# A gated-attention and mixture kernel: where the D parts of the hidden tiles are made, and how attention units overlap

## Chip, core and metric

The kernel runs on one core of a Trainium2 chip. The metric is the device time of one execution in microseconds. Before the change it is 1072.71 us, the median of three runs from 1072.09 to 1073.56.

## What is computed

The first half is a gated linear recurrence. For each of 4 batches and 8 heads, over 768 positions of dimension 48:

```
state = alpha[t][:, None] * state + outer(k[t], v[t])
y[t]  = q[t] @ state
```

The second half takes y as 3072 rows of 384 numbers and runs four experts over all of them:

```
p = domain_probs / (domain_probs.sum(-1) + 1e-9)
for e in range(4):
    h = max(x @ w1[e], 0)            # 384 -> 1024
    out += p[:, e] * (h @ w2[e])     # 1024 -> 384
```

Everything is in fp32.

## The kernel before

**Attention units.** The recurrence is done in blocks of 128 positions. One block of one batch is a unit, attention(u), and there are 24 of them, ordered by block first and batch second. attention() is a generator of 17 steps (0 to 16), and each `yield` ends one. Steps 0 to 2 transpose alpha, k and q (`tp`), and step 1 also forms the products q*k (`own`, `dot`). Steps 3 to 6 begin the levels of a doubling scheme: ScalarE copies q (copy_q), VectorE multiplies q, the decay and k (next_q, next_k). Step 6 also fills the diagonal tile `near`. Step 7 makes the first scores, 32 matmuls on levels 0 to 3, and VectorE takes the results over masks (take). Steps 8 to 10 continue the levels. Step 11 makes the last scores (`far` and two more levels). Steps 12 and 13 copy `far` and `near` into `lat`. Step 14 transposes the keys back into AT. Step 15 is result(): matmuls on `lat`, v, q and the state into `yps`, copied to x_raw. Step 16 updates the state: matmuls into `sps`, then two VectorE operations on each half of the partitions. From the first block to the last but one a unit has such an update.

**Groups and experts.** The units are put in seven groups: the first two units, five groups of four, the last two. Group gi of the mixture covers the rows of its units. In this text gi is counted from 0. While the experts of group gi run, the attention units of the next group are worked on; while group 4 runs, the units of groups 5 and 6. The experts of groups 5 and 6 run without attention beside them.

**Layer 1.** up(gi, e, fc) makes one of eight hidden tiles of 128 features by up to 512 rows. From group 1 on, weights and x are split in three parts, so that fast matmuls give nearly fp32 results: six matmuls into `one` and three into `two`, in a ring of four PSUM banks. ScalarE scales `one` into t and VectorE adds `two` (L553). From group 2 on, the hidden tile is split as well (hidden_parts): ScalarE makes the top part, VectorE the low part (L580), and make_dif the D part, top/4096 - low (L590). These steps are put behind the matmuls of the next tile, so on VectorE the order is low and D of tile k-1, then the addition of tile k.

**D parts before.** With 512 rows, hidden_parts makes D for the first 256 columns at once, in layer 1. The second 256 go to the queue `later`, which down() empties.

**Layer 2.** down(gi, e, slots, between) multiplies hidden tiles with w2. From group 2 on, one call takes two slots of 128 rows, so a full group needs two calls, here called first and second. A call has 48 matmuls, n = 0 to 47: n = 0 to 31 use the top and low parts, tiles 0 to 5 ahead of 6 and 7, and n = 32 to 47 use the D parts, the eight tiles of the first slot and then those of the second. At each n with n % 4 == 3 one entry of `later` is made. add_up() accumulates the sums: for the first slot behind n = 29 and n = 39, for the second behind n = 31 and n = 47. In expert 0 the accumulation behind n = 29 and n = 31 is ScalarE's. In the last expert of a group, split_x() for the next group stands between the matmuls: ScalarE's part at the start of the first call, three pairs of VectorE operations (L248, L249) at n = 2, 12 and 22 of the second.

**The order.** It is written out by hand (manual_schedule), and every engine runs its instructions in the order of the program. A planner decides where attention steps go: up() and down() advance a clock by an estimated cost (advance, cost), and deal() gives each step of each unit a due time on that clock. deal() gives the units of a group an equal `space`, lets a unit last twice that, and puts its steps at the shares of its duration that BEATS lists. wanted[gi] is the moment when group gi's rows must be there, and MARGIN is kept ahead of it.

The buffers that bind steps of neighbouring units are `near` and `lat` (one each), the decay tile of the last level dec6 (one), four blocks of q, five tiles KT, and in PSUM two banks for scores, two for `tp`, `yps` and `sps`, four for the mixture.

Of the kernel before, what the change touches and what calls it, by code (L numbers as in the profile page):

```python
# [10 lines left out]
F32 = mybir.dt.float32  # L11
# [9 lines left out]
def kernel(  # L21
# [37 lines left out]
    nc = tc.nc  # L59

    B, H, S, D = q.shape
    E, DM, F = moe_w1.shape
    P = 128
    NCB = S // P
    NP = H // 2
    HD = 64
# [4 lines left out]
    NT = B * P  # L71
# [10 lines left out]
    j = np.arange(P)[:, None] % HALF  # L82
    n = np.arange(QUAD)[None, :]
# [7 lines left out]
    work = ctx.enter_context(tc.tile_pool(name="work", bufs=2))  # L91
    hid = ctx.enter_context(tc.tile_pool(name="hid", bufs=2))
    ps = ctx.enter_context(tc.tile_pool(name="ps", bufs=2, space=bass.MemoryType.PSUM))
# [18 lines left out]
    half = B // 2  # L112
    groups = [order[:half]] + [order[i:i + B] for i in range(half, len(order), B)]
    LAST = len(groups) - 1
# [16 lines left out]
    def raw(u, nm):  # L131
        return values[u % 2] if nm == "v" else apart[nm] if u == 1 else early[nm]
# [6 lines left out]
    splitting = []  # L139
    stores = deque()  # L140
    late = deque()
    later = deque()
    shared = {}
    accs = {}


    BEATS = [*(0.055 * (j + 1) for j in range(11)), 0.69, 0.75, 0.8, 0.87, 0.94, 1.0]
    MARGIN = 6.0
    waiting = deque()
    clock = 0.0  # L150
# [109 lines left out]
    def halves(t, m):  # L260
        return t.rearrange("p a (b two r) -> p a b two r", two=2, r=m)
# [7 lines left out]
    def attention(u):  # L269
        cb, b = units[u]  # L270
        ra, rk, rq, rv = (raw(u, nm) for nm in ("a", "k", "q", "v"))
# [39 lines left out]
        def next_q(li):  # L311
            m = LEVELS[li]
            qv = halves(QT, m)[:, :, :, 1, :]
            dv = halved(decs[li])
            nc.vector.tensor_mul(qv, qv, spread(dv[:, :, :, 0], m))  # L315
            dec = work.tile([P, NP, P // (2 * m)], F32, name=f"dec{li}", bufs=1)
            nc.vector.tensor_mul(dec, dv[:, :, :, 0], dv[:, :, :, 1])
            decs.append(dec)

# [33 lines left out]
        for li in range(3):  # L353
            copy_q(li)
            next_q(li)
            next_k(li)
            yield
# [29 lines left out]
        for r in range(NP // 2):  # L387
            for s in range(2):
                nc.tensor.matmul(far[HALF * s:HALF * (s + 1), r],  # L389
                                 lhsT=KTs[6][:, 2 * r + s, :HALF], rhs=qbs[6][:, 2 * r + s],  # L390
                                 start=True, stop=True)
# [7 lines left out]
        parts = lat.rearrange("p (r s i) c -> p r s i c", s=2, i=2)  # L399
        for s in range(2):  # L400
            rows = slice(HALF * s, HALF * (s + 1))
            nc.scalar.copy(out=parts[:HALF, :, s, :, HALF:], in_=far[rows])
        yield
        for s in range(2):
            rows = slice(HALF * s, HALF * (s + 1))
# [4 lines left out]
        st = sts[b]  # L410
# [47 lines left out]

        if cb < NCB - 1:
            KB = AT  # L460
            sps = ps.tile([P, NP, 2, D], F32, name="sps", tag="w")
            for p in range(NP):
                nc.tensor.matmul(sps[:, p], lhsT=KB[:, p, :], rhs=rv[:, 2 * p:2 * p + 2, :D],  # L463
                                 start=True, stop=True)
            for i in range(2):
                rows = slice(HD * i, HD * (i + 1))
                old, add = st[rows, :, i, :], sps[rows, :, i, :]
                if cb == 0:
                    nc.vector.tensor_copy(out=old, in_=add)
                else:  # L470
                    nc.vector.tensor_mul(old, old, decs[-1][rows].broadcast_to([HD, NP, D]))
                    nc.vector.tensor_add(old, old, add)
# [103 lines left out]
    def hidden_parts(x, parts):  # L576
        top, low, dif = parts
        nc.scalar.activation(out=top, in_=x, func=ACT.Relu, scale=TRIM)  # L578
        yield
        nc.vector.scalar_tensor_tensor(out=low, in0=x, scalar=0.0, in1=top.bitcast(F32),  # L580
                                       op0=ALU.max, op1=ALU.subtract)

        n = x.shape[-1]
        at = n // 2 if n == NT else 0
        if at:
            make_dif(*(part[:, :at] for part in parts))
        later.append([part[:, at:] for part in parts])

    def make_dif(top, low, dif):
        nc.vector.scalar_tensor_tensor(out=dif, in0=top.bitcast(F32), scalar=1 / 4096.0,  # L590
                                       in1=low.bitcast(F32), op0=ALU.mult, op1=ALU.subtract)
# [5 lines left out]
    def down(gi, e, slots, between):  # L597


        first = first_piece(gi, e)  # L600
        halves_ = split2(gi, e)
        if slots[0] == 0 and makes[1](gi, e):
            making.extend(split_piece(1, first + k) for k in range(NQ))
        if slots[0] == 0 and makes[0](gi, e) and 0 < e < E - 1:
            making.extend(split_piece(0, first + k) for k in range(2, NQ))
        sums = [[ps.tile([P, DM], F32, name=f"ops{j}", tag="g", bufs=4)
                 for j in range(2 if halves_ else 1)] for _ in slots]

        kinds = [((0, 1), range(FCH - 2)), ((0, 1), range(FCH - 2, FCH)), ((2,), range(FCH))]
        steps = [(part, i, fc) for parts, tiles in (kinds if halves_ else [((3,), range(FCH))])  # L610
                 for part in parts for i in range(len(slots)) for fc in tiles]
        for n, (part, i, fc) in enumerate(steps):
            c, f = divmod(fc, FPQ)
            h = hidden[c][:, :, f, slots[i] * P:(slots[i] + 1) * P]
            advance(cost(1, gi, e) / FCH / (3 if halves_ else 1))
            while between and n >= between[0][0] * len(steps):
                between.popleft()[1]()
            if n == len(steps) // 2:
                background()
            if later and n % 4 == 3:  # L620
                make_dif(*later.popleft())
            if halves_:
                w = wt[1][first + c].rearrange("p t (c d) -> p t c d", d=DM)[:, part, f]
                nc.tensor.matmul(sums[i][part // 2], lhsT=h[:, part], rhs=w,  # L624
                                 start=(fc == 0 and part != 1), stop=(fc == FCH - 1 and part != 0))
            else:
                w = wt[1][first + c].rearrange("p (c d) -> p c d", d=DM)[:, f]
                nc.tensor.matmul(sums[i][0], lhsT=h[:, 2].bitcast(F32), rhs=w,  # L628
                                 start=(fc == 0), stop=(fc == FCH - 1))
            if part >= 1 and fc == FCH - 1:  # L630
                add_up(gi, e, slots[i], part // 2, sums[i][part // 2 if halves_ else 0])
        while between:
            between.popleft()[1]()
        background()
        if slots[-1] == len(groups[gi]) - 1 and gi != LAST - 1:
            while makes[1](gi, e) and (making or splitting):
                background()

            for c in range(NQ):
                del wt[1][first + c]  # L640
                if c < NQ // 2 or gi == LAST:
                    load_piece(1, first + NQ + c)
                else:
                    late.append(first + NQ + c)
# [25 lines left out]
    def cost(layer, gi, e):  # L670
        n = len(groups[gi]) / 4
        if layer == 0:
            return 2.1 * n if split1(gi, e) else 2.6 * n
        return 4.1 if split2(gi, e) else 5.4

    def deal():

        wanted = [0.0]  # L680
        ends = [0.0, 0.0]
        events = []
        t = 0.0
        for (gi, e), after in zip(tasks, tasks[1:]):
            part = 1 - 1 / len(groups[0]) if gi == e == 0 else 1
            t += cost(0, gi, e) * FCH * part
            if after[1] == 0:
                wanted.append(t)
            t += cost(1, gi, e) * len(groups[gi]) * part

        for gis in [*([gi] for gi in range(1, LAST - 1)), [LAST - 1, LAST]]:
            gi, due = gis[0], wanted[gis[-1]] - MARGIN
            n = sum(len(groups[i]) for i in gis)
            first = wanted[gi - 1] if gi > 1 else 0.0
            space = (due - first) / (n if gi > 1 else (n + 1) / 2)
            if gi == 1:
                space /= 2
            for k in range(n):
                u = sum(map(len, groups[:gi])) + k
                end = due - (n - 1 - k) * space  # L700
                begin = max(end - 2 * space, ends[-2])
                ends.append(end)
                run = attention(u)
                events += [(begin + (end - begin) * beat, u, run) for beat in BEATS]
        return sorted(events, key=lambda x: x[:2])

    def advance(spent):
        nonlocal clock
        clock += spent
        while waiting and clock >= waiting[0][0]:  # L710
            next(waiting.popleft()[2], None)

    with tc.manual_schedule():
# [48 lines left out]
        for (gi, e), after in zip(tasks, [*tasks[1:], (None, None)]):  # L762
# [6 lines left out]
            for k, slots in enumerate(turns):  # L769

                between = deque()
                if after[1] == 0:
                    for step, at in enumerate((0.0, 0.52, 0.62, 0.72)):
                        at = at * len(turns) - k
# [33 lines left out]
```

## Time and profile before

| | before |
|---|---|
| median of three runs | 1072.71 us |
| the profiled execution | 1073.32 us |
| its span, first to last instruction | 1071.6 us |
| mean granted TensorE clock | 0.998 |
| groups 2, 3, 4 of the mixture, with attention | 374.6 to 880.5 us |
| VectorE busy in group 2, 3, 4 | 132.75 of 166.1, 136.25 of 169.5, 133.33 of 170.3 us |

A row of the profile's groups gives line, engine, operation, what is written and read, shapes, count, then busy time and mean duration, then idle time ahead of it and what ended that. Timeline rows begin with the start in us and the time the merged instructions take; in square brackets stands an idle time ahead and its releaser. Rows of waits read: engine, waiting tile and line, what it waited for, total us, how often, the longest. TensorE matmuls overlap, so the distance between starts is what one costs, not its duration, and an fp32 matmul shows as two records.

### The profile page before, as it was taken

What the parts mean: (1) busy time and instruction counts of PE and PEld (TensorE: products, weight loads), DVE (VectorE), ACT (ScalarE), POOL (GpSimd) and SP (SyncE); (2) the same over time, 40 slices, a digit from 0 to 9 for tenths busy, and PEclk for the clock granted to TensorE, in tenths of its full rate; (3) what the DMA queues carried; (4) which work ended last, traced back from release to release, by engine and by line L of the source; (5) the groups of instructions that cost most, each with busy time, mean ns of one, the idle gap of its engine ahead of it and who ended that gap; (6) DMA issues with size and microseconds to landing.
All of it is one profiled execution on the core that took longest, in us unless ns stands there. A gap on an engine that the chain in (4) does not pass through costs nothing.

```text
span 1071.6 us, 21614 instructions
## 1 busy us (share of the span) xinstructions
PE 1048.1 (98%) x8460; PEld 899.1 (84%) x8460; DVE 775.2 (72%) x1711; ACT 566.7 (53%) x1202; POOL 32.7 (3%) x71
## 2 busy tenths in 40 slices
PE   8899999999999999999999999999999999999998
PEld 8777777676776798898898898898889889898988
DVE  5488776656566978778877777986787866666565
ACT  5687866575656554536546445555464543323232
POOL 2010000000000100000000000000000000000000
PEclk9999999999999999999999999999999999999999
DMA  8597699687696967758759558586594543544540
GB/s 123 156 330 216 230 328 368 238 328 241 236 309 209 402 216 274 281 160 312 268 170 359 204 187 337 186 281 234 158 358 173 221 192 147 207 177 178 187 181 31
DMA packets 158838, 251.67 MB, mean 235 GB/s; under 512 B 120112, under 2 KB 135344, under 8 KB 136208
## 3 DMA queue, kind: packets, MB, share of 16 engines
q1 hardware_dynamic: 149600, 208.82, 57.1%
q0 software_dynamic: 5760, 41.29, 9.8%
q8 instruction: 67, 1.10, 0.4%
q10 hardware_dynamic: 3376, 0.17, 0.3%
q14 instruction: 35, 0.29, 0.1%
HBM read 207.79 MB, written 42.47 MB: 234 GB/s over the span
## 4 chain that ended last, share of the span: by engine, by line
PE 83%; DVE 8%; ACT 6%; issue 2%; DMA 1%; SPq 0%; DVEq 0%; ACTq 0%
PE ops L624 25%; PE one L540 21%; PE ops L628 10%; PE two L540 10%; PE sc L334 6%; PE yps L428 3%; PE tp L266 3%; PE one L532 2%; ACT qb L308 2%; PE far L389 1%; PE sps L463 1%; DVE near L344 1%; DVE t L553 1%; DVE hT L580 1%; DVE hT L590 1%
## 5 line engine op out<-in xcount | busy, mean ns | idle before, releaser
L624 PE MATMUL ops<-w,hT 128*128 128x384 f32 x1728 | 318.0, 339 | 4.4 <-DVE acc L658 4.3
L624 PEld LDWEIGHTS ops<-w,hT 128*128 128x128 f32 x1728 | 299.1, 188 | 9.9 <-DVE acc L658 5.6
L540 PE MATMUL one<-xT,w 128*128 128x512 f32 x960 | 253.8, 400 | 2.6 <-DVE xT L248 1.1
L540 PEld LDWEIGHTS one<-xT,w 128*128 128x128 f32 x960 | 176.3, 188 | 41.8 <-DVE QT L315 1.6
L551 ACT ACTIVATE t<-one 128x512 f32<-128x512 f32 (+1 forms) x192 | 106.3, 554 | 153.6 <-PE one L540 148.5
L308 ACT COPY qb<-QT 64x256 f32<-64x256 f32 x336 | 136.4, 406 | 77.0 <-DVE QT L289 44.1
L578 ACT ACTIVATE hT<-t 128x512 fp32r<-128x512 f32 (+1 forms) x160 | 94.3, 589 | 123.6 <-DVE t L553 122.9
L580 DVE SCALAR_TENSOR_TENSOR hT<-t,hT 128x512 fp32r<-128x512 f32 (+1 forms) x160 | 102.2, 638 | 55.7 <-ACT hT L578 53.6
L540 PE MATMUL two<-xT,w 128*128 128x512 f32 x480 | 136.7, 393 | 0.0
L628 PE MATMUL ops<-hT 128*128 128x384 f32 x384 | 133.4, 491 | 0.0
L553 DVE TENSOR_TENSOR t<-t,two 128x512 f32<-128x512 f32 (+1 forms) x160 | 100.8, 630 | 41.9 <-ACT t L551 21.4
L590 DVE SCALAR_TENSOR_TENSOR hT<-hT 128x256 fp32r<-128x256 f32 x288 | 111.9, 422 | 4.4
L540 PEld LDWEIGHTS two<-xT,w 128*128 128x128 f32 x480 | 90.6, 189 | 20.0
L628 PEld LDWEIGHTS ops<-hT 128*128 128x128 f32 x384 | 69.5, 190 | 40.1 <-issue 0.4
L315 DVE TENSOR_TENSOR QT<-QT,dec 128x256 f32<-128x256 f32 x144 | 60.8, 422 | 38.2 <-ACT qb L308 37.5
L344 DVE COPY_PREDICATED near<-masks,sc 128x256 f32<-128x256 uint8 x144 | 77.0, 535 | 15.5 <-PE sc L334 12.8
L334 PEld LDWEIGHTS sc<-qb,KT 128*64 128x64 f32 x2304 | 72.7, 138 | 9.7 <-issue 5.6
L334 PE MATMUL sc<-qb,KT 128*64 128x64 f32 x2304 | 77.2, 223 | 2.6 <-ACT qb L308 2.6
L658 DVE SCALAR_TENSOR_TENSOR acc<-ops,p_all,acc 128x384 f32<-128x384 f32 x82 | 49.5, 614 | 33.9 <-PE ops L624 14.5
L326 ACT COPY KT<-KT 128x256 f32<-128x256 f32 x144 | 59.9, 416 | 3.2
L327 DVE TENSOR_TENSOR KT<-KT,dec 128x256 f32<-128x256 f32 x144 | 60.3, 419 | 0.0
L558 DVE TENSOR_TENSOR hT<-t,two 128x512 f32<-128x512 f32 x32 | 22.0, 688 | 35.6 <-ACT t L551 23.0
(88 smaller groups left out, 970.7 us busy)
## 6 DMA issues: line engine op xcount, KB each, us to landing
w<-kept SPq DMA_DIRECT2D x144, 1152.0 KB
kept<-w POOLq DMA_DIRECT2D x32, 1152.0 KB, 7.4
hT<-in_moe_w_dram SPq DMA_DIRECT2D x32, 384.0 KB
w<-in_moe_w_dram SPq DMA_DIRECT2D x48, 128.0 KB
ra<-in_alpha_dram SPq DMA_DIRECT2D x23, 192.0 KB
rk<-in_k_dram SPq DMA_DIRECT2D x23, 192.0 KB
rq<-in_q_dram SPq DMA_DIRECT2D x23, 192.0 KB
out_dram<-acc POOLq DMA_DIRECT2D x18, 192.0 KB, 6.6
```

Source lines behind the costliest of these rows:

```text
L308: nc.scalar.copy(out=qb[rows, :, i, :].rearrange("p a (b r) -> p a b r", r=m), in_=qv[rows])
L315: nc.vector.tensor_mul(qv, qv, spread(dv[:, :, :, 0], m))
L334: nc.tensor.matmul(out[HALF * s:HALF * (s + 1), 2 * p:2 * p + 2, :], lhsT=KTs[li][:, p, HALF * s:HALF * (s + 1)], rhs=qbs[li][:, p, :, QUA ...
L344: nc.vector.copy_predicated(near.rearrange("p a (b two r) -> p a b two r", two=2, r=m)[:, :, :, 1, :], mk.unsqueeze(1).broadcast_to([P, H, ...
L540: nc.tensor.matmul(out, lhsT=w[:, part, kc], rhs=x_part(gi, part, kc), start=(part == terms[0] and kc == 0), stop=(part == terms[-1] and k ...
L551: nc.scalar.activation(out=t, in_=one, func=ACT.Copy, scale=FINE)
L553: nc.vector.tensor_add(t, t, two)
L578: nc.scalar.activation(out=top, in_=x, func=ACT.Relu, scale=TRIM)
L580: nc.vector.scalar_tensor_tensor(out=low, in0=x, scalar=0.0, in1=top.bitcast(F32), op0=ALU.max, op1=ALU.subtract)
L590: nc.vector.scalar_tensor_tensor(out=dif, in0=top.bitcast(F32), scalar=1 / 4096.0, in1=low.bitcast(F32), op0=ALU.mult, op1=ALU.subtract)
L624: nc.tensor.matmul(sums[i][part // 2], lhsT=h[:, part], rhs=w, start=(fc == 0 and part != 1), stop=(fc == FCH - 1 and part != 0))
L628: nc.tensor.matmul(sums[i][0], lhsT=h[:, 2].bitcast(F32), rhs=w, start=(fc == 0), stop=(fc == FCH - 1))
```

## The change

Four things are changed.

1. hidden_parts makes no D part. It puts one entry of 256 columns into each of two queues, and a call of down() empties the queue of its own two slots, one entry at each n % 4 == 3. In the last group, with 256 rows, there is one queue and nothing changes.
2. Units from number 10 on (those of group 3 and later) get their steps by IN_PAIRS instead of BEATS. Step 7 of a unit is given the very time of step 15 of the unit ahead, and step 11 that of step 16 of the unit ahead, where these lie within a sixth of the space. The other steps are spread between. Step 6 is kept behind step 13 of the unit ahead, and step 12 behind its step 15.
3. The state update of units 9 to 19 is computed in two halves of 64 rows and 48 columns per pair of heads, in place of one matmul of 128 rows and 96 columns of which half was read. dec6 gets a second buffer.
4. In deal() the windows of groups 3 and 4 begin earlier by MARGIN.

```diff
-    later = deque()
+    later = [deque(), deque()]
...
+    IN_PAIRS = [*(0.0425 * (j + 1) for j in range(8)), 0.385, 0.43, 0.475, 0.52, 0.6, 0.67, 0.755, 0.84, 1.02]
+    TOGETHER = ((15, 7), (16, 11))
+    pairs_from = half + 2 * B
...
-            dec = work.tile([P, NP, P // (2 * m)], F32, name=f"dec{li}", bufs=1)
+            dec = work.tile([P, NP, P // (2 * m)], F32, name=f"dec{li}", bufs=1 + (li == 6))
...
-            sps = ps.tile([P, NP, 2, D], F32, name="sps", tag="w")
+            apart_ = u + 1 >= pairs_from
+            sps = ps.tile([P, NP, 1 if apart_ else 2, D], F32, name="sps", tag="w")
             for p in range(NP):
-                nc.tensor.matmul(sps[:, p], lhsT=KB[:, p, :], rhs=rv[:, 2 * p:2 * p + 2, :D],
-                                 start=True, stop=True)
+                for i in range(2) if apart_ else [slice(0, 2)]:
+                    rows = slice(HD * i, HD * (i + 1)) if apart_ else slice(0, P)
+                    nc.tensor.matmul(
+                        sps[rows, p], lhsT=KB[:, p, rows],
+                        rhs=rv[:, 2 * p + i, :D] if apart_ else rv[:, 2 * p:2 * p + 2, :D],
+                        start=True, stop=True)
             for i in range(2):
                 rows = slice(HD * i, HD * (i + 1))
-                old, add = st[rows, :, i, :], sps[rows, :, i, :]
+                old, add = st[rows, :, i, :], sps[rows, :, 0 if apart_ else i, :]
...
-        n = x.shape[-1]
-        at = n // 2 if n == NT else 0
-        if at:
-            make_dif(*(part[:, :at] for part in parts))
-        later.append([part[:, at:] for part in parts])
+        for k in range(0, x.shape[-1], 2 * P):
+            later[k // (2 * P)].append([part[:, k:k + 2 * P] for part in parts])
...
-            if later and n % 4 == 3:
-                make_dif(*later.popleft())
+            dif = later[slots[0] // 2]
+            if dif and n % 4 == 3:
+                make_dif(*dif.popleft())
...
-            first = wanted[gi - 1] if gi > 1 else 0.0
+            first = wanted[gi - 1] - MARGIN * (2 < gi < LAST - 1) if gi > 1 else 0.0
...
-                events += [(begin + (end - begin) * beat, u, run) for beat in BEATS]
+                pairs = u >= pairs_from
+                beats = [0.0, *(IN_PAIRS if pairs else BEATS)]
+                due_at = {-1: begin, **{j: begin + (end - begin) * beats[j + 1] for j in (7, 11, 16)}}
+                for ahead, j in TOGETHER if pairs else ():
+                    if (u > pairs_from or j == 11) and abs(times[-1][ahead] - due_at[j]) < space / 6:
+                        due_at[j] = times[-1][ahead]
+
+                marks = sorted(due_at)
+                times.append([])
+                for lo, hi in zip(marks, marks[1:]):
+                    times[-1] += [due_at[hi] if j == hi else
+                                  due_at[lo] + (due_at[hi] - due_at[lo]) * (beats[j + 1] - beats[lo + 1])
+                                  / (beats[hi + 1] - beats[lo + 1]) for j in range(lo + 1, hi + 1)]
+
+                for j, ahead in ((6, 13), (12, 15)):
+                    if times[:-1]:
+                        times[-1][j] = max(times[-1][j], times[-2][ahead] + 0.5)
+                events += [(time, u, run) for time in times[-1]]
```

More of the change, by code (lines that the diff above doesn't have):

```diff
@@ L682, in deal @@
         events = []
+        times = []
         t = 0.0
```

## The prediction

> **What bounds the kernel now.** First the page: engine shares, the chain that ended last, the costliest groups.
>
> ```profile
> PE 1048.1 (98%) x8460; PEld 899.1 (84%) x8460; DVE 775.2 (72%) x1711; ACT 566.7 (53%) x1202; POOL 32.7 (3%) x71
> ...
> PE 83%; DVE 8%; ACT 6%; issue 2%; DMA 1%; SPq 0%; DVEq 0%; ACTq 0%
> ...
> L624 PE MATMUL ops<-w,hT 128*128 128x384 f32 x1728 | 318.0, 339 | 4.4 <-DVE acc L658 4.3
> ...
> L590 DVE SCALAR_TENSOR_TENSOR hT<-hT 128x256 fp32r<-128x256 f32 x288 | 111.9, 422 | 4.4
> ```
>
> TensorE sets the end. What can change is its instruction stream, or the moments in which it waits for VectorE. The span to look at is 374.6 to 880.5 us, groups 2, 3 and 4 (gi from 0), where the split second layer and attention units run together. The waits of that window:
>
> ```profile
> DVE hT L580 <- ACT hT L578: 33.7, 48, 1.1
> ...
> PEld ops L624 <- DVE acc L658: 5.6, 4, 2.2
> ```
>
> So TensorE stopped four times in layer 2, for an accumulation on VectorE. By starts of successive matmuls these stops cost 0.64, 0.66, 2.07 and 1.60 us (at 592, 676, 763 and 850 us), 5.0 together; one of 0.65 us at 833 us in layer 1 comes on top. That is all a faster VectorE could give. The stop at 850 us, TensorE and then VectorE:
>
> ```profile
> 848.84 1.57 PE L624 MATMUL ops<-w,hT 128*128 128x384 f32 x8
> 851.84 0.97 PE L624 MATMUL ops<-w,hT 128*128 128x384 f32 x4 [1.43 <-DVE acc L658]
> ...
> 850.17 1.09 DVE L590 SCALAR_TENSOR_TENSOR hT<-hT 128x256 fp32r<-128x256 f32 x3
> 851.17 0.61 DVE L658 SCALAR_TENSOR_TENSOR acc<-ops,p_fine,acc 128x384 f32<-128x384 f32 x1
> 851.70 0.42 DVE L590 SCALAR_TENSOR_TENSOR hT<-hT 128x256 fp32r<-128x256 f32 x1
> ```
>
> VectorE is still making D parts of the first call of down() when TensorE stands at the second. It arrives late in layer 2 because of a loop in layer 1, seen best where no attention runs:
>
> ```profile
> 926.41 0.43 DVE L590 SCALAR_TENSOR_TENSOR hT<-hT 128x256 fp32r<-128x256 f32 x1
> 926.75 0.68 DVE L553 TENSOR_TENSOR t<-t,two 128x512 f32<-128x512 f32 x1
> 928.13 0.69 DVE L580 SCALAR_TENSOR_TENSOR hT<-t,hT 128x512 fp32r<-128x512 f32 x1 [0.70 <-ACT hT L578]
> 928.86 0.42 DVE L590 SCALAR_TENSOR_TENSOR hT<-hT 128x256 fp32r<-128x256 f32 x1
> ```
>
> One turn (t, ScalarE's top, low, D) takes 2.45 us; TensorE needs 9 matmuls at 0.229 = 2.06. Over 8 tiles VectorE falls some 3 us behind.
>
> [...] The trace [...] shows 0.34 us from start to start in a run of D parts. [...] the D part at 851.70 stands behind the accumulation at 851.17 though its inputs were long there. [...] Here 'far' behind 'ops' starts 0.268 us after it instead of 0.174[...]; a result and first scores cost 1.763 and 2.104 us apart, 3.775 in a row, again 0.09 less.
>
> **The change part by part.** Prices are start-to-start times of the profiled run.
>
> *State product in halves.* Now and after:
>
> ```profile
> 410.92 1.02 PE L463 MATMUL sps<-rv,AT 128*128 128x96 f32 x8
> 411.73 1.63 PE L540 MATMUL one<-xT,w 128*128 128x512 f32 x6
> ...
> 424.81 1.10 PE L334 MATMUL sc<-qb,KT 128*64 128x64 f32 x32
> 425.84 0.62 PE L624 MATMUL ops<-w,hT 128*128 128x384 f32 x2
> ```
>
> Each fp32 matmul shows as two records. 8 records of sps take 0.81 us. After: 16 records on 64-column halves with 48 columns. The nearest row, sc, has equal weights and 64 columns: 0.030 each (1.03 us for 32, of which 0.09 is the exit). So 16 x 0.028 = 0.45; bounds 0.38 (48/64 of the row) and 0.48. Gain 0.36. Units 9 to 19 have it: 11 x 0.36 = -4.0 us. The two VectorE operations per half read the same 64x192: nothing.
>
> *Last scores behind the state update.* One interruption less in 11 units, 0.09 each: -1.0. First scores behind the result: 10 of 13 such pairs are in a row already; three more give -0.3. The matmuls themselves move, none is added; loads of a, k, q, v move with their steps on SP's queue, by under 3 us of a 40 us period, and no wait on them is among the long ones now. The second dec6 buffer adds no instruction, and the wider spacing of units in groups 3 and 4 (34.5 and 33.2 planner units apart instead of 33.0 and 31.7) only spreads the same work: nothing.
>
> *D parts.* Still 16 of 256 columns per group and expert. 8 leave layer 1: the loop becomes 2.45 - 0.34 = 2.11, level with TensorE, and the tail of layer 1 ends about 2.3 us after layer 2 begins instead of 4.7 to 5.9. That takes the 5.0 and the 0.65 away: -5.6 us, covered by VectorE being 2.5 to 3 us earlier at each of the four stops (largest 2.07).
>
> But the first call's parts were made long ahead, and the second's one call ahead. Now each call makes its own at n = 3, 7 ... 31 of 48 matmuls and reads them from n = 32; D7, made at 31, is due at n = 39. Between stand acc (0.53) behind matmul 29 and D7 itself (0.42 plus some 0.3 until the accumulation sees its matmul): 1.25 of the 10 x 0.174 = 1.74. Half a microsecond is left, and whatever VectorE does late there now stops TensorE. Group 6 works so already, without attention: 0.
>
> First calls. Until D7 VectorE has: tail 2.3, D 8 x 0.34 = 2.75, acc 0.53, and by the planner's formulas steps 2 and 3 of the unit behind (0.62 + 1.0) and often step 1's products (1.0) out of layer 1: 8.2. TensorE is at n = 39 after 39 x 0.174 = 6.8 plus 0.36 for a transpose: 7.15. Late by 1.0 by sum, 0.6 when laid out in order (step 1's transpose delays layer 2 too). In expert 0 the first accumulation is ScalarE's: 0.5 less. Over 12 calls I take eight at 0.5: +4.0; bounds 0 and 9.
>
> Second calls without a split: from the first's last matmul 0.3 + acc 0.53, D 2.75, acc 0.53, steps 4 to 6 (0.85 + 0.8 + 0.6): 6.4 against 7.15. Nothing, or 0.3 once or twice: +0.5.
>
> Second calls of expert 3 also hold the split of the next group's x, three times this pair:
>
> ```profile
> 680.24 0.68 DVE L248 TENSOR_TENSOR xT<-x_raw,xT 128x512 fp32r<-128x512 f32 x1
> 680.95 0.69 DVE L249 SCALAR_TENSOR_TENSOR xT<-xT 128x512 fp32r<-128x512 f32 x1
> ```
>
> 3 x 1.32 = 3.95. Now VectorE is busy there without a gap and nobody waits. After: 0.3 + 0.53 + 2.75 + 0.53 + 3.95 = 8.06 plus attention. Group 2: steps 4 and 5, 1.65, so 9.7 against 7.15: 2.5. Group 3: steps 3, 4, 5, 2.65, so 10.7: 3.5. Group 4: none, against 6.8: 1.3. Together +7.3; bounds 3 (each a microsecond and a half earlier) and 11.
>
> After each stop the next matmul showed another 0.09 to 0.11: some 12 stops, +1.3.
>
> Sum: -4.0 - 1.0 - 0.3 - 5.6 + 4.0 + 0.5 + 7.3 + 1.3 = +2.2 us. On the span of 1071.6 (1.7 us of the run's 1073.3 lie around it) that is 1073.8, on the median of 1072.7 it is **1075**, 0.2% slower.
>
> **Rivals.**
> *Faster:* VectorE keeps up. Its total does not grow, 133 of 166 us busy in group 2, and gaps of 33.7 us behind ScalarE's top can take attention work. If the new stops stay at 5 us, -10.9 + 5 = -6: 1067. It decides where they sum to less than 8.8. For it: without attention the margin is positive; against: the split calls, where there is no gap to use.
> *Much slower:* steps emitted at n = 28 to 31 (3, 7, 5, by the plan in half of the calls) hold D7 up with their own waits for ScalarE or for scores, 0.75 each in 24 calls, 18 instead of 4.5 with the splits unchanged: +15, 1083 to 1087 at the top. Against: ScalarE is half idle, and results and scores inserted just there cost TensorE 3.8 us, which gives VectorE time.
> *No effect of the merging:* the halves do not overlap and sps costs 16 x 0.055 = 0.88. Then -4.0 becomes +0.8: 1080. Against: sc and far overlap in the same form.
>
> **How the numbers follow.** Within 0.2% (2.1 us: what a measurement of this kernel tells from no change) is 1070.6 to 1074.9. Forecast, stops of 9 to 18 us: 0.50, own range 1071 to 1080, of which 0.31 slower and 0.19 within. Faster rival 0.33, of which 0.03 within. Much slower 0.10; halves without overlap 0.07, of which 0.02 within. So faster 0.30, same 0.24, slower 0.46. The range for 8 in 10 is 1066 to 1082: the forecast, the faster rival but for its end, the lower part of the slower ones.
>
> **What would show it.** Right: sps in 16 records of about 0.03 us, in a row with far; the layer 1 loop at 2.1 us; new waits of ops for the D part (line of make_dif) at the last third of calls, longest in the second call of expert 3; none left for the accumulation. Wrong: no waits of ops for D over 0.3 us, or D7 done before n = 39 in the split calls; then the kernel is faster.

## The result

The changed kernel takes 1086.97 us (median of four runs, 1085.21 to 1089.62) against 1073.13 us for the one before: a ratio of 1.0132, interval 1.0109 to 1.0155. It is 13.8 us slower, where 2.2 us slower was forecast. The profiled execution took 1085.21 us with a span of 1083.4, so the two traces differ by 11.8 us. They do not have the same clock, though. Below is one stretch of the trace of before; columns: stretch, length, busy time of TensorE matmuls, weight loads, VectorE, ScalarE, GpSimd, then the granted TensorE clock, the DMA share and GB/s:

```profile
167.43:170.84 3.41, 3.41 (x10) 2.63 (x10) 1.32 (x3) 1.63 (x4) 0.54 (x1) 0.50 1.01 427
```

For these 3.41 us TensorE had half its clock, which cost some 1.7 us (half of the stretch, an estimate). The trace of the changed kernel has no such stretch (mean clock 1.000), so at full clock the two would be 13.5 us apart, close to the 13.8 us of the medians.

The page of the changed kernel, engine shares and the two costliest groups of layer 2:

```profile
PE 1048.5 (97%) x8548; PEld 891.9 (82%) x8548; DVE 769.4 (71%) x1711; ACT 570.7 (53%) x1202; POOL 32.9 (3%) x71
...
L632 PE MATMUL ops<-w,hT 128*128 128x384 f32 x1728 | 319.4, 341 | 11.8 <-DVE hT L597 11.8
...
L597 DVE SCALAR_TENSOR_TENSOR hT<-hT 128x256 fp32r<-128x256 f32 x288 | 105.1, 418 | 0.0
```

TensorE's busy time did not grow: its 88 more records are the halves. VectorE is busy 6 us less, ScalarE 4 us more with the same 1202 instructions. TensorE's idle time is what grew. Its waits from 374.6 to 895 us:

```profile
PE ops L632 <- DVE hT L597: 11.8, 16, 2.6
PE far L394 <- DVE hT L590: 2.7, 1, 2.7
PE far L394 <- ACT qb L313: 1.2, 1, 1.2
```

L597 is make_dif. The four waits for an accumulation are gone, and sixteen for a D part stand in their place; the last scores (`far`) wait twice. By starts of successive matmuls (less the usual distance) the D waits sum to 15 us: 8.4 in eight first calls, 6.0 in the second calls of expert 3, 0.6 in one other second call.

The longest one shows more than the prediction had laid out. ScalarE and VectorE in the first call of group 3, expert 0, with TensorE's return:

```profile
552.00 0.58 ACT L664 ACTIVATE acc<-ops,p_fine 128x384 f32<-128x384 f32 x1 [3.54 <-PE ops L632]
552.48 1.23 ACT L411 COPY lat<-near 64x512 f32<-64x512 f32 x2
553.72 0.84 ACT L313 COPY qb<-QT 64x256 f32<-64x256 f32 x2
...
554.59 0.43 DVE L320 TENSOR_TENSOR QT<-QT,AT 128x256 f32<-128x256 f32 x1 [2.53 <-ACT qb L313]
...
555.61 0.42 DVE L597 SCALAR_TENSOR_TENSOR hT<-hT 128x256 fp32r<-128x256 f32 x1
...
556.08 1.13 PE L632 MATMUL ops<-w,hT 128*128 128x384 f32 x5 [2.56 <-DVE hT L597]
```

VectorE is idle for 2.53 us with D7 in its queue. Ahead of D7 stands step 3's multiplication of q, which waits for ScalarE's copy of q; that copy stands behind a copy of `near` (step 13, due at the same clock), which stands behind an accumulation that waits for TensorE.

The stop of `far`, at the start of layer 2 in group 3, expert 3:

```profile
671.67 1.20 PE L632 MATMUL ops<-w,hT 128*128 128x384 f32 x6
675.54 0.66 PE L394 MATMUL far<-qb,KT 128*64 128x128 f32 x8 [2.67 <-DVE hT L590]
...
672.71 0.58 ACT L561 ACTIVATE t<-one 128x512 f32<-128x512 f32 x1
674.15 0.63 ACT L588 ACTIVATE hT<-t 128x512 fp32r<-128x512 f32 x1 [0.87 <-DVE t L563]
674.69 0.80 ACT L313 COPY qb<-QT 64x256 f32<-64x256 f32 x2
```

Step 11 stands six matmuls into layer 2. The copy of q from step 10 that it reads is behind ScalarE's part of the last hidden tile, which VectorE releases late. The wait put down to L590 is this copy's; TensorE's weight loads name it:

```profile
PEld far L394 <- ACT qb L313: 4.5, 2, 3.0
```

The loop of layer 1 did what was forecast; VectorE in group 5, without attention:

```profile
932.28 0.69 DVE L563 TENSOR_TENSOR t<-t,two 128x512 f32<-128x512 f32 x1
933.67 0.69 DVE L590 SCALAR_TENSOR_TENSOR hT<-t,hT 128x512 fp32r<-128x512 f32 x1 [0.70 <-ACT hT L588]
934.38 0.69 DVE L563 TENSOR_TENSOR t<-t,two 128x512 f32<-128x512 f32 x1
```

One turn takes 2.10 us instead of 2.45. But TensorE's own rate is not the old one. Layer 1 there, TensorE in the changed kernel, one hidden tile of nine matmuls from row 1 to row 3:

```profile
936.21 1.56 PE L550 MATMUL one<-xT,w 128*128 128x512 f32 x6
937.61 0.86 PE L550 MATMUL two<-xT,w 128*128 128x512 f32 x3
938.31 1.56 PE L550 MATMUL one<-xT,w 128*128 128x512 f32 x6
```

and in the kernel before:

```profile
924.92 1.53 PE L540 MATMUL one<-xT,w 128*128 128x512 f32 x6
926.29 0.85 PE L540 MATMUL two<-xT,w 128*128 128x512 f32 x3
926.98 1.53 PE L540 MATMUL one<-xT,w 128*128 128x512 f32 x6
```

A tile takes 2.10 us against 2.06. From start to start such a matmul takes 232 ns in the median and 233.4 on the mean, instead of 229 to 230, in every stretch from 160 us on, also where the change reorders nothing. What did change there are addresses: the second dec6 buffer moves xT, x_raw, the hidden tiles and acc up by 32 bytes in each partition.

### The profile page after: what moved, and what is told of

The parts are those of the page before. It is cut to its first block, busy times and chain, and to the rows that moved or that the text cites. A ratio compares the mean times of both kernels' runs of the same rounds, so it can differ in the third digit from the quotient of the medians.

```text
span 1083.4 us, 21812 instructions
## 1 busy us (share of the span) xinstructions
PE 1048.5 (97%) x8548; PEld 891.9 (82%) x8548; DVE 769.4 (71%) x1711; ACT 570.7 (53%) x1202; POOL 32.9 (3%) x71
## 5 line engine op out<-in xcount | busy, mean ns | idle before, releaser
L632 PE MATMUL ops<-w,hT 128*128 128x384 f32 x1728 | 319.4, 341 | 11.8 <-DVE hT L597 11.8
L590 DVE SCALAR_TENSOR_TENSOR hT<-t,hT 128x512 fp32r<-128x512 f32 (+1 forms) x160 | 102.0, 638 | 54.3 <-ACT hT L588 53.0
L597 DVE SCALAR_TENSOR_TENSOR hT<-hT 128x256 fp32r<-128x256 f32 x288 | 105.1, 418 | 0.0
L542 PE MATMUL one<-xT,w 128*128 128x256 f32 (+1 forms) x240 | 46.0, 340 | 0.6 <-ACT xT L449 0.6
```

## Experiments

Four causes had to be told apart: the addresses, the D parts, the new order of attention, and the state product. In x2, x4, x6, x9 and x10 the addresses of before were kept by putting the second dec6 buffer behind all tiles; x3, x5, x7 and x8 start from the kernel before and move no tile.

### x1_layout: the addresses alone

```diff
-            dec = work.tile([P, NP, P // (2 * m)], F32, name=f"dec{li}", bufs=1)
+            dec = work.tile([P, NP, P // (2 * m)], F32, name=f"dec{li}", bufs=1 + (li == 6))
```

> The kernel before with one thing alone: the second buffer of dec6, which is never used to advantage here but moves every later tile (xT, x_raw, the hidden tiles, acc) up by 32 bytes in each partition. Theory 'addresses': the matmuls of layer 1 are slower by 3 to 4 ns each because xT starts at a multiple of 64 bytes (and of 4096) now; 1440 of them from 160 us on, so +4 to +6 us, and the start-to-start time of a 512-column matmul is 232 to 233 ns instead of 229. Theory 'order alone': no change, within 1 us of before.

1075.84 us against 1073.75 for the kernel before, measured beside it: ratio 1.0018 (1.0010 to 1.0026), 2.1 us slower. Among runs of the same mean clock the difference is 2.4 us (0.998) and 3.0 us (1.000). Layer 1 takes 232 ns per matmul in all stretches (233.4 on the mean). So the move alone costs time, and the theory "order alone" falls; the size is half of what was expected. By the traces layer 1 lost 4 ns per matmul, 5.8 us over 1440, and layer 2 won about 1 ns in the stretch with attention (175.0 to 174.1 on the mean), some 1 us over 1153 matmuls. The rest of the difference is not accounted for.

### x2_same_addr: the changed kernel at the old addresses

```diff
+    tail = ctx.enter_context(tc.tile_pool(name="tail", bufs=1))
...
-            dec = work.tile([P, NP, P // (2 * m)], F32, name=f"dec{li}", bufs=1 + (li == 6))
+            pool = tail if li == 6 and u % 2 else work
+            dec = pool.tile([P, NP, P // (2 * m)], F32, name=f"dec{li}", bufs=1)
```

> The changed kernel with the second dec6 buffer put behind all other tiles, so that every tile of before has its old address. Theory 'addresses': 512-column matmuls back at 229 ns, 4 to 6 us faster than the changed kernel, so 1081 to 1083 us. Theory 'order alone': same as the changed kernel, 1086 to 1087 us.

1084.13 us, ratio 1.0107 (1.0090 to 1.0123), with layer 1 back at 229 to 230 ns. That is 2.8 us under the changed kernel, which was measured on another occasion; the two intervals overlap. The direction is as expected, the size again smaller, but these runs had lower clocks too (0.993 to 0.998 against 0.995 to 1.000). Some 10 us remain for the order and the D parts.

### x3_d_only: the D parts alone, on the kernel before

The diff of hidden_parts and down() as in the change, nothing else.

> The kernel before with the D parts beside the second layer alone, addresses and attention order of before. Theory 'D due at n = 39': the four waits for an accumulation go, new waits for D come, 3 us and more in second calls of expert 3, 10 to 16 us in all, so +4 to +10 us: 1077 to 1083. Theory 'the new attention order makes the waits': without it D is ready, 1066 to 1070 us.

1086.79 us, ratio 1.0127 (1.0112 to 1.0141): 13 us slower, more than expected. The rival (without the new order D is ready in time) is out. The waits of TensorE's weight loads:

```profile
PEld ops L622 <- DVE hT L587: 17.9, 25, 1.9
```

Twenty-five waits, most of them short. With the old order the D parts do more harm (13 us) than with the new one, where they add 2.5 us (x2_same_addr less x4_pairs_only, below).

### x4_pairs_only: the new order and the halves, D parts as before

The changed kernel at the old addresses, with hidden_parts and down() of before.

> The changed kernel with the D parts as before (half in layer 1, the rest one call ahead), old addresses; the new attention order, the state product in halves and the earlier windows stay. Theory 'D due at n = 39': its 15 us of waits for D go; waits for the accumulation come back, 2 to 5 us; the state product gives 3.7 us: 1069 to 1074. Theory 'the new order is the loss': 1078 or more.

1081.59 us, ratio 1.0070 (1.0054 to 1.0085). A time of 1069 to 1074 was expected; the new order, with the halves and the earlier windows, loses 7.8 us without any D part moved. The waits of weight loads name the place:

```profile
PEld far L396 <- ACT qb L314: 8.4, 3, 5.6
PEld ops L636 <- DVE acc L670: 7.7, 7, 2.1
```

The stop of `far` in group 3 is longer here, since layer 1 carries D parts and leaves ScalarE and VectorE later. And slow clock came behind it. Two stretches of this run, with the columns as above:

```profile
670.00:676.00 6.00, 1.53 (x9) 1.13 (x7) 5.19 (x12) 1.97 (x5) 0.00 (x0) 1.00 0.97 306
676.00:682.00 6.00, 5.18 (x55) 5.03 (x56) 4.13 (x12) 2.83 (x7) 0.00 (x0) 0.72 0.01 5
```

TensorE stood for 5.28 us, and the clock of the next 6 us was 0.72. Here too the clock is half for 3.41 us, from 676.3 us on. The trace has four such stretches (two follow a stop of `far`), that of x2_same_addr has two, behind stops of 2.6 and 2.7 us, and the changed kernel's has none behind equal stops (2.67 and 2.72 us, mean clock 1.000). The one before the change follows two shorter stops, of 1.0 and 1.1 us. So such a stretch came behind some stops and not behind others of the same length; what brings it on was not shown. Each costs some 1.7 us (half of 3.41, an estimate). By the mean clocks, 0.995 in the middle of these six runs against 0.998 before, about 3 of the 7.8 us are clock (an estimate).

### x5_halves: the state product in halves alone

The diff of the state update, with pairs_from, in the order of before.

> The kernel before with the state product in halves alone (units 9 to 19), attention order and addresses of before. sps should take 0.45 us in 16 records instead of 0.81 in 8, but alone between matmuls of another tiling it also pays about 0.09 us on entering and 0.09 on leaving: 11 x 0.18 = 2 us faster, 1071 to 1073. Rival 'halves do not overlap': 16 x 0.055 = 0.88 us and the two changes of mode, 11 x 0.25 = 3 us slower.

1073.18 against 1073.36 us, ratio 1.0002 (0.9993 to 1.0011): no difference that can be told, where 2 us were expected. The halves do overlap: the 16 records take 0.60 us, not the 0.88 of the rival, whose 0.055 for a record was an estimate. So the rival is out. TensorE around one update:

```profile
408.60 0.85 PE L546 MATMUL two<-xT,w 128*128 128x512 f32 x3
409.38 0.67 PE L467 MATMUL sps<-rv,AT 128*64 128x48 f32 x16
409.98 1.66 PE L546 MATMUL one<-xT,w 128*128 128x512 f32 x6
```

From the start of the three `two` matmuls to sps 0.78 us pass instead of 0.68, sps takes 0.60 instead of 0.81, and the six matmuls behind it 1.50 instead of 1.47: a net gain of 0.08, 0.9 us over 11 units. Joined with the last scores, as in the change, sps, far and scores take 2.083 us instead of 0.810 + 1.613, which is 0.34 less. The matmul behind sps, slowed before (0.316 us to the next start instead of 0.229), now coincides with the one behind the scores, 0.09 more: 0.43 for each joined unit. Ten of the eleven units are joined in the changed kernel; the eleventh gains 0.09.

### x6_far_later: last scores not joined to the state update

On x4_pairs_only:

```diff
-    IN_PAIRS = [*(0.0425 * (j + 1) for j in range(8)), 0.385, 0.43, 0.475, 0.52, 0.6, 0.67, 0.755, 0.84, 1.02]
-    TOGETHER = ((15, 7), (16, 11))
+    IN_PAIRS = [*(0.0425 * (j + 1) for j in range(8)), 0.385, 0.43, 0.475, 0.61, 0.65, 0.7, 0.755, 0.84, 1.02]
+    TOGETHER = ((15, 7),)
```

> x4_pairs_only with the last scores (step 11) no longer joined to the state update of the unit ahead: they stand at 0.61 instead of 0.52 of the unit's time, which leaves some 6 us more behind step 10. Theory 'last scores are sent before ScalarE has copied the last q': the waits of far, 8 us in x4_pairs_only, fall to under 1 and the time by 4 to 8 us, to 1074 to 1078. Theory 'VectorE is short whatever the order': far waits go, accumulation waits grow by as much, 1080 to 1083.

1076.36 us, ratio 1.0023 (1.0014 to 1.0031): 5.2 us less than x4_pairs_only. The 8.4 us of waits for the copy of q are gone, those for the accumulation stay:

```profile
PEld ops L636 <- DVE acc L670: 6.9, 8, 1.9
```

The clocks are higher too, 0.998 to 1.000 against 0.993 to 0.997, so a part of the 5.2 us is clock. The joining is what made `far` wait; it gave some 0.34 us ten times and took more at two places.

### x7_d_sooner: D parts at every third matmul

On x3_d_only:

```diff
-            if dif and n % 4 == 3:
+            if dif and n % 3 == 2:
```

> x3_d_only with the D parts made at n = 2, 5 ... 23 of a call instead of 3, 7 ... 31, so that the last has eight matmuls (1.4 us) more until it is due. Theory 'D7 is due half a microsecond behind': stops of 0.4 to 1.3 us go, those of the split calls stay, 6 to 9 us faster than x3_d_only, 1077 to 1081. Theory 'VectorE lacks throughput in layer 2': the stops move to earlier D parts or to accumulations and the time stays within 2 us of x3_d_only.

1076.57 us, ratio 1.0033 (1.0022 to 1.0045): 10.2 us less than x3_d_only, with the same work. The waits halve:

```profile
PEld ops L622 <- DVE hT L587: 8.8, 15, 1.5
```

So it is not throughput that VectorE lacks in most calls. It was the place of the D parts, the last one eight matmuls ahead of its use and behind an accumulation, that cost some 10 us. What stays is largest in the second calls of expert 3.

### x8_d_own_call: half of the D parts in layer 1, the other half in their own call

On the kernel before:

```diff
...
-        later.append([part[:, at:] for part in parts])
+        later[int(at > 0 and e < E - 1)].append([part[:, at:] for part in parts])
...
-            if later and n % 4 == 3:
-                make_dif(*later.popleft())
+            dif = later[slots[0] // 2]
+            if dif and n % 4 == 3:
+                make_dif(*dif.popleft())
```

> The kernel before with half of the D parts in layer 1 as before, the other half in the second call instead of the first, except in expert 3, where the split stands in the second call and they stay in the first. Theory 'what hurts is D in the first call, right behind layer 1, and D beside the split': few new stops, the four waits for an accumulation partly gone, 1068 to 1074. Theory 'any D part made in its own call stops TensorE': half of x3_d_only's loss, 1077 to 1082.

1073.72 us, ratio 0.9998 (0.9990 to 1.0007): as fast as before. Second calls of experts 0 to 2 have room for D parts; one wait for D of 1.0 us came, three of the four accumulation waits stayed. This gains nothing by itself.

### x9_both: both causes mended

The changed kernel at the old addresses with the edits of x6_far_later and x7_d_sooner.

> The changed kernel at the old addresses with both suspected causes mended: D parts at n = 2, 5 ... 23, and the last scores (step 11) at 0.61 instead of joined to the state update. Theory: the accumulation waits of x6_far_later (12 us) go because layer 1 has no D part, the D waits of x7_d_sooner (9 us, mainly split calls) stay: 1068 to 1074. Rival 'order and D parts collide in some other way': 1077 or more.

1068.44 us against 1073.43 us, ratio 0.9958 (0.9944 to 0.9971): 5 us faster than the kernel before. Neither edit was tried alone on the changed kernel. Nearly all that is left of TensorE's waits:

```profile
PEld ops L634 <- DVE hT L599: 5.0, 6, 1.5
```

The parts do not add up singly: x7_d_sooner is 3.2 us slower than before and x6_far_later 3.0 us. Together the D parts leave layer 1, so that the accumulation waits of x6_far_later go.

### x10_split_spared: expert 3 as before

On x9_both:

```diff
...
-        for k in range(0, x.shape[-1], 2 * P):
-            later[k // (2 * P)].append([part[:, k:k + 2 * P] for part in parts])
+        n = x.shape[-1]
+        at = n // 2 if n == NT and e == E - 1 else 0
+        if at:
+            make_dif(*(part[:, :at] for part in parts))
+        for k in range(at, n, 2 * P):
+            later[0 if at else k // (2 * P)].append([part[:, k:k + 2 * P] for part in parts])
```

> x9_both with expert 3 as before the change: half of its D parts in layer 1, the other half in the first call, none in the second, where the split of x stands. Theory 'the split calls have no room for D': 3 to 6 us faster than x9_both, 1066 to 1071, and no wait of ops for D over 0.5 us in the last expert of a group. Rival 'the room is found elsewhere': same as x9_both, with accumulation waits in expert 3 in their place.

1067.89 us, ratio 0.9943 (0.9930 to 0.9955), 0.5 us under x9_both where 3 to 6 were expected; the two cannot be told apart. The D waits of the split calls are gone, but others came in expert 3:

```profile
PEld ops L638 <- DVE t L565: 2.2, 2, 1.8
...
PEld ops L638 <- DVE acc L672: 1.4, 2, 0.9
```

The rival holds here: beside the split VectorE is short of time, and moving its D parts to layer 1 moves the wait. This is the lowest median found.

### x11_up_96 and x12_hidden_32: which tile, which address

In x11_up_96 xT and all behind it move up by 96 bytes, by a wider dec6; in x12_hidden_32 only the hidden tiles and acc move, by 32.

```diff
-            dec = work.tile([P, NP, P // (2 * m)], F32, name=f"dec{li}", bufs=1)
+            if li < 6:
+                dec = work.tile([P, NP, P // (2 * m)], F32, name=f"dec{li}", bufs=1)
+            else:
+                dec = work.tile([P, 32], F32, name="dec6", bufs=1)[:, :NP].unsqueeze(2)
```

```diff
-                    xraws[gi] = work.tile([P, KC, NT], F32, name="x_raw", bufs=1)
+                    xraws[gi] = work.tile([P, KC * NT + 8], F32, name="x_raw", bufs=1)[:, :KC * NT].rearrange(
+                        "p (k n) -> p k n", n=NT)
```

> The kernel before with xT, x_raw, the hidden tiles and acc moved up by 96 bytes in each partition instead of 32, so that xT starts at a multiple of 64 but not of 4096. Theory '64 bytes': a 512-column matmul of layer 1 takes 232 to 233 ns from start to start as in x1_layout. Theory '4096 bytes': 229 as before.

> The kernel before with the hidden tiles and acc moved up by 32 bytes, xT where it was. Theory 'it is xT': layer 1 at 229 ns as before; layer 2 may go from 174 to 173 as in x1_layout. Theory 'it is the hidden tiles': layer 1 at 232 to 233 ns.

One run each: 1080.60 and 1073.56 us. With 96 bytes a 512-column matmul takes 234 ns on the mean in every stretch and one of layer 2 176 to 177; with the hidden tiles alone moved, layer 1 stays at 229 and layer 2 is at 173 to 174. So in these layouts layer 1 follows the address of xT and layer 2 that of the hidden tiles. The theory "4096 bytes" as put falls: at a multiple of 64 that is not one of 4096 layer 1 is slowest. The theory "64 bytes" stands for layer 1, on three addresses, but not for layer 2, where the fastest and the slowest are both multiples of 64. A rule for good addresses does not follow from four layouts.

## Why the prediction was wrong

By its own steps, on the profiled execution:

- **State product in halves, -4.0, and one interruption less, -1.0:** right. Ten joined units gave 0.43 us and one 0.09, -4.4 together. The halves alone, not joined, gave nothing that can be told (x5_halves).
- **First scores behind the result, -0.3:** one more pair stands in a row, not three: -0.1.
- **Last scores behind the state update, with nothing for a wait:** this failed. The prediction priced the joining of step 11 by the 0.09 us of one interruption saved, said that matmuls and loads only move, and did not ask what step 11 reads. Step 10's copy of q is on ScalarE behind layer 1's tail, and `far` waited 2.7 and 1.3 us: +4.0. x6_far_later shows the cause by 5.2 us, a part of it clock, in the form without the D parts.
- **"The second dec6 buffer adds no instruction", nothing:** failed as well. It moved xT by 32 bytes, and x1_layout gives +2.4 to +3.0 us for that at like clock.
- **D parts, relief -5.6:** right. The four accumulation waits and the stop at 833 us are gone, and the loop of layer 1 takes 2.10 us as worked out (2.11).
- **First calls, +4.0:** mis-sized, 8.4. Eight calls stop, as taken, but all of them for more than 0.5 us: five for 0.63 to 0.78, the others for 0.98, 1.28 and 2.72. The 2.72 was the mechanism of the slower rival, a step at n = 30 or 31 that waits for ScalarE. "ScalarE is half idle" spoke against it; ScalarE's share of the span said nothing of what stood ahead of that copy in its queue. In the stops of 0.98 and 1.28 VectorE was not idle: an attention step stood ahead of D7 there too, and its own work took the time.
- **Split calls, +7.3:** 1.5, 3.4 and 1.1 us where 2.5, 3.5 and 1.3 were forecast: 6.0. Other second calls 0.6 for 0.5. Right. x10_split_spared shows that moving these D parts into layer 1 does not win the time back: other waits come in their place.
- **Resuming, +1.3:** the matmuls behind the new stops took 1.2 us more than those behind the old ones. Right.

Taken together, with 2.7 for the addresses: -4.4 - 0.1 - 5.6 + 4.0 + 2.7 + 8.4 + 6.0 + 0.6 + 1.2 = +12.8, against the 13.5 us by which the spans differ at full clock. The remaining 0.7 is not traced to a step. The forecast's 2.2 lacked 4.4 us of the first calls, 4.0 of `far` and 2.7 of the addresses, had 0.8 too much of a gain in the state product and the scores, and had the split calls 1.3 too high.

The range ended at 1082 because the slower rival was given one chance in ten. The rival's time, 1083 to 1087, is what came, by a mixture of its mechanism and two that no case held. What the forecast said decides, new stops summing to less than 8.8 us, agrees with x9_both: with 5.0 us of them the kernel is 5 us faster, near the 1067 of the faster rival. That they meet so closely is in part luck, since x9_both does not join the last scores and so lacks most of the -5.0 that the rival counted on.

## What to carry to other kernels

Work that is made just ahead of its use has a due time on the consumer; compare that with everything queued ahead of it on its engine, and with what those instructions wait for on a third engine (2.53 us of VectorE's idle time ahead of one D7). A few matmuls more of lead (x7_d_sooner: 8 of them, 10.2 us) can be worth more than the waits that the move was to remove (5.6 us). When two steps are joined, ask for the last input of the joined step, not only for the interruption saved. And a buffer that is added can move other tiles (the second dec6 buffer moved xT by 32 bytes, 2.4 to 3.0 us in x1_layout at like clock): keep addresses fixed when order is to be judged, and compare runs, and traces above all, at the same mean clock (0.998 instead of 1.000 went with 2.0 us in the kernel before).

## What was not expected of the hardware

The rate of a matmul stream depended on where its SBUF operand starts. Means from start to start: layer 1, 512 columns, xT at 147424 bytes in the partition: 229 to 230 ns; at 147456: 233.4; at 147520: 234. Layer 2, 384 columns, with attention beside it, first hidden tile at 172000: 175 ns; at 172032: 173 to 174; at 172096: 176 to 177. The address is not all: at 147424 the last stretch of x4, x6, x7 and x9 shows 230.4 and that of the others 229. In the 96-byte case a single run of the whole kernel was 7 us over the median before.

The slow clock came in stretches of 3.41 us at 0.50, none to four in a trace. One of them in the trace of before is a mean clock of 0.998, and they go with most of the spread of one kernel's times: at 0.998 the kernel before took 1073.9 us in the median of ten runs, at 1.000 it took 1071.9 in the median of five (the runs beside x1_layout).
